# A fused attention and long-convolution kernel: SBUF laid out on two stacks, work paired anew, DRAM writes moved to another queue

## The chip, the cores and the metric

The program runs on one core of one Trainium2 chip. The time is device time in microseconds (us) of one execution. All executions counted here were fast; two slow ones are left out. Each kernel was timed in at least three rounds beside the kernel before, on the same chip. The engines are called PE (TensorE, matrix products), DVE (VectorE), ACT (ScalarE), POOL (GpSimd) and SP (SyncE, which here only issues DMAs). PEld is the loading of PE's weights, which overlaps its products.

## The reference

Two independent halves are computed and joined. Sequence length S is 2048, width D is 576, everything in bf16.

```python
def A(x, wqkv, wo):                 # 32 heads of 18; 8 taps, 2 apart
    q, k, v = split_heads(x @ wqkv)
    kg, vg = k[:, :, idx], v[:, :, idx]        # idx = pos - 2 * (0..7)
    logits = einsum("bhsd,bhswd->bhsw", q, kg) * scale   # masked where idx < 0
    o = einsum("bhsw,bhswd->bhsd", softmax(logits), vg)
    return merge_heads(o) @ wo

def B(q, k, v, shift_k, ssm_k, ssm_D):
    kv = short_conv_4_taps(k, shift_k) * v
    y = irfft(rfft(kv, 2S) * rfft(ssm_k, 2S))[:S]   # a long convolution
    return q * (y + kv * ssm_D)

return concatenate([A(...), B(...)], axis=-1)
```

## The kernel before

The kernel writes both halves as *steps* and emits them in pairs with `run(a, b)`, which interleaves two lists of steps. A scheduler at compile time then fixes the order of instructions on every engine; at run time each engine executes its own list strictly in that order, waiting where an input isn't there yet.

The steps that matter are these.

- `v_step` (16 of them) and `qk_step` (18 with the two half steps) project x: PE, then one ACT copy out of PSUM.
- `k_step` (8) makes the first half of the Fourier transform of the kernel `ssm_k`: PE transposes, one DVE copy into `kTt`, products (`L262`), ACT copies, and a write to DRAM (`Dk`).
- `x_step` (8): the four-tap convolution on DVE (`kv_step`, which makes `tA` for two x steps), then the same products, to `Dx`.
- `logit_step` (8): q times shifted k on DVE (`prod`), summed by head on PE, then one ACT copy (`Lsb`).
- `g_step` (8): reads `Dk` and `Dx`, second half of both transforms (`Kc`, `Xc`), their complex product on DVE (`m`), first half of the inverse transform, written to `Dy`.
- `pv_step` (8): attention weights times v on DVE (`P`), sum and output projection on PE.
- `y_step` (8): reads `Dy`, last half of the inverse transform, times q, output.

```python
    vX = const.tile([128, 30, D], BF16, name="vX")
    ...
    nc.gpsimd.memset(vX[0:1, 0:14, :], 0.0)                  # one partition
    ...
        # end of s1_chunk, the tail of k_step and x_step
        for ri in range(2):
            nc.scalar.dma_start(by_f1(Dd)[:, ri, 2 * c2:2 * c2 + 2, :], vst[...])
    ...
    permute_wv()                                             # on GpSimd
    a_steps = v steps + q/k steps
    run(a_steps[0:12], [k_step(c2) for c2 in range(8)])
    kpre_v.release(); kpre.release()
    kvp = pool("kvp", 2, "right")           # the convolution's buffers lie here
    run(a_steps[12:], [sk_step] + [x_step(c2) for c2 in range(8)])
    ...
    run([logit_step(wi) for wi in range(W)] + [softmax_step]
        + [at_step(wp) for wp in range(4)],
        [ia_tables] + [g_step(g) for g in range(3)])
    ...
    run([pv_step(tp) for tp in range(5)], [g_step(g) for g in range(3, 8)])
    run([pv_step(tp) for tp in range(5, 8)], [y_step(c2) for c2 in range(8)])
```

The convolution's buffers are allocated on the space that the `k_step` buffers give back. This is the point that the change is about.

## Time and profile before

The median is 333.05 us (332.08 to 333.26). The table of windows cuts the profiled execution (span 330.3 us) into stages; each engine's column is its busy time in that stretch, and the last three columns are the clock granted to PE (1.00 is full), the busy share of the DMA engines, and GB/s. Stages of the kernel before: set-up; v beside k steps; the k steps run out; convolution; logits with three g steps; softmax; PV; tail.

```profile
core 0: us, PE busy (x) PEld busy (x) DVE busy (x) ACT busy (x) POOL busy (x), PEclk, DMA share, GB/s
0.00:27.00 27.00, 9.63 (x81) 8.41 (x82) 21.27 (x30) 6.81 (x7) 19.95 (x32) 0.92 0.62 200
27.00:70.00 43.00, 40.18 (x290) 32.98 (x290) 6.06 (x8) 26.34 (x38) 0.00 (x0) 0.97 0.38 131
70.00:88.00 18.00, 16.84 (x77) 7.73 (x79) 1.36 (x1) 8.82 (x10) 1.53 (x1) 1.00 0.92 275
88.00:123.00 35.00, 29.54 (x154) 13.66 (x154) 34.02 (x26) 20.52 (x25) 0.00 (x0) 0.95 0.60 204
123.00:180.00 57.00, 34.37 (x319) 13.14 (x318) 55.02 (x42) 23.43 (x37) 2.85 (x4) 0.73 0.42 133
180.00:205.00 25.00, 12.13 (x96) 7.45 (x96) 21.24 (x19) 18.19 (x27) 9.33 (x20) 0.66 0.43 127
205.00:289.00 84.00, 76.11 (x909) 54.16 (x909) 57.40 (x35) 53.18 (x88) 0.00 (x0) 0.98 0.30 100
289.00:330.00 41.00, 23.12 (x207) 16.13 (x204) 13.98 (x17) 5.67 (x9) 3.26 (x6) 0.83 0.77 245
```

Read it down the PE and DVE columns. From 27 to 88 us PE is busy 57 of 61 us and DVE 7.4. From 123 to 180 us it is the other way round: DVE is busy 55 of 57 us, PE 34, and at a granted clock of 0.73. The Trainium skill ("TensorE: Matmul & The Clock Gate", What's actually happening) says that PE's clock is throttled by default and that activity releases it; from 27 us on the table agrees: 0.73 and 0.66 where PE is busy 34 of 57 and 12 of 25 us, 0.97 to 1.00 where it is busy 57 of 61. The two engines take turns, and the sum of the turns is the time.

A word on the clock column. Each figure is a mean over stretches recorded at 1.00 or 0.50, and time without a record counts as 1.00. The set-up's figures are therefore no measurement: the first record comes at 19.2 us here.

The waits of DVE from 27 to 125 us say why it idles. The columns are the engine, what it wants to run, what it waits for, then total us, times and the longest.

```profile
DVE kTt L288 <- PE psB L285: 34.8, 8, 11.0
DVE skb L326 <- DMA tB<-in_B_shift_k_dram: 16.9, 1, 16.9
```

The first convolution instruction, the copy of `shift_k` (`skb`), comes after all eight k steps, and then waits 16.9 us more for its load, which could be issued only when the k steps' buffers were free.

The set-up has a smaller oddity, seen in the timelines of DVE (first line) and of GpSimd (second line): start, duration, instruction.

```profile
4.94 6.81 DVE L138 TENSOR_SCALAR n_132<-g_130,p_f 128x128 int32<-128x128 int32 x2
```

```profile
4.76 6.84 POOL L191 MEMSET vX<- 1x8064 bf16 x1
```

A table instruction of 128x128 elements takes as long as the clearing of 8064 elements in one partition on another engine.

### The profile page before, as it was taken

To read this page: it belongs to the slowest core of one execution; us is meant where nothing else is said; L and a number is where in the kernel's file an instruction comes from. 1 tells how busy PE (TensorE), PEld (TensorE's weight loads), DVE (VectorE), ACT (ScalarE), POOL (GpSimd) and SP (SyncE) were. 2 spreads that over 40 slices of the span, in tenths; PEclk is the share of its full clock that TensorE was granted. 3 is DMA by queue.
4 is the path that set the end of the run, shared out by engine and by line. 5 is a ranking of instruction groups with operands and counts; after the bars stand their busy time and mean duration, and the time that the engine had idled before them with its cause. 6 is when DMAs were issued, how large, how long until landed. Compare 5 with 4: busy or idle time off the path is not lost.

```text
span 330.3 us, 5054 instructions
## 1 busy us (share of the span) xinstructions
PE 241.9 (73%) x2125; PEld 153.7 (47%) x2129; DVE 210.3 (64%) x175; ACT 163.0 (49%) x236; POOL 36.9 (11%) x61
## 2 busy tenths in 40 slices
PE   2349999879997874385657166999998978876732
PEld 2237876744443331032213034775766555665411
DVE  5981011100499999999997888977558663733431
ACT  1223567764446664072527587457756668431200
POOL 9950000010000000000004900000000000001110
PEclk9987999999997997569858557799999999999965
DMA  7907044459927836029604542162524201159993
GB/s 267 274 23 269 0 145 143 146 198 267 354 51 256 286 127 193 21 81 296 197 2 143 144 135 91 73 163 105 165 109 144 109 36 73 38 167 334 302 302 113
DMA packets 28355, 52.36 MB, mean 159 GB/s; under 512 B 2286, under 2 KB 22446, under 8 KB 28205
## 3 DMA queue, kind: packets, MB, share of 16 engines
q1 hardware_dynamic: 16156, 33.53, 32.1%
q10 hardware_dynamic: 10912, 15.34, 12.7%
q0 software_dynamic: 1264, 3.17, 3.8%
q8 instruction: 16, 0.26, 0.3%
q14 instruction: 7, 0.06, 0.0%
HBM read 31.11 MB, written 18.87 MB: 151 GB/s over the span
## 4 chain that ended last, share of the span: by engine, by line
issue 38%; DVE 26%; PE 15%; DMA 11%; ACT 4%; POOL 3%; SPq 1%; DVEq 0%; POOLq 0%
DVE prod L377 6%; PE psA L218 4%; DVE tB L343 4%; DVE tA L348 4%; DMA qt<-in_B_q_dram 3%; ACT vst L266 3%; PE psB L262 3%; DMA kX<-in_B_k_dram 3%; PE psB L285 2%; DVE n_132 L138 2%; DMA Wk<-Dy 2%; DVE W_73 L167 2%; DVE tA L343 2%; DVE stageB L543 2%; PE psA L202 1%
## 5 line engine op out<-in xcount | busy, mean ns | idle before, releaser
L505 DVE TENSOR_TENSOR P<-vX,at 128x4608 bf16<-128x4608 bf16 x16 | 40.3, 2554 | 20.6 <-PE psA L514 19.4
L514 PE MATMUL psA<-ident,P 128*128 128x128 bf16 (+1 forms) x640 | 46.3, 222 | 0.0
L266 ACT ACTIVATE vst<-psB 128x768 bf16<-128x768 f32 x48 | 36.6, 810 | 17.9 <-PE psB L262 17.3
L514 PEld LDWEIGHTS <-P 128*128 128x128 bf16 (+1 forms) x640 | 38.6, 101 | 9.7 <-issue 7.5
L231 PE MATMUL psA<-xT,wq 128*128 128x512 bf16 x156 | 37.1, 387 | 2.4 <-ACT vX L220 1.4
L288 DVE COPY kTt<-psB 128x1152 bf16<-128x1152 bf16 x8 | 6.1, 757 | 34.8 <-PE psB L285 34.8
L481 ACT ACTIVATE Y<-psB 128x576 bf16<-128x576 f32 x32 | 19.1, 652 | 16.3 <-PE psB L478 16.3
L536 POOL DMA_DIRECT2D qt<-in_B_q_dram x8 | 4.3, 544 | 201.3 <-DVE stageB L543 120.9
L543 DVE TENSOR_TENSOR stageB<-psB,qt 128x576 bf16<-128x576 f32 x16 | 11.4, 753 | 22.9 <-PE psB L542 10.4
L527 PE MATMUL psA<-wot,oT 128*128 128x288 bf16 x160 | 22.8, 287 | 3.9 <-ACT oT L520 3.0
L218 PE MATMUL psA<-wv,xT 128*128 128x288 bf16 x160 | 24.2, 297 | 1.9 <-ACT vX L220 1.3
L231 PEld LDWEIGHTS <-wq 128*128 128x128 bf16 x160 | 15.9, 99 | 20.8 <-issue 3.3
L380 PE MATMUL psA<-prod,Eh 128*32 128x512 bf16 x128 | 14.2, 489 | 14.8 <-DVE prod L377 14.7
L435 ACT ACTIVATE Kc<-psB 128x576 bf16<-128x576 f32 x32 | 19.8, 649 | 6.4 <-PE psB L432 3.9
L542 PE MATMUL psB<-Wk,IB 128*128 128x288 bf16 x64 | 12.9, 323 | 13.5 <-DMA Wk<-Dy 11.9
L432 PEld LDWEIGHTS <-W_73 128*64 128x64 bf16 x256 | 14.2, 116 | 17.5 <-issue 15.2
L218 PEld LDWEIGHTS <-xT 128*128 128x128 bf16 x160 | 20.4, 146 | 3.5 <-ACT xT L205 0.9
L202 PE MATMUL psA<-ident,xnat 128*128 128x128 bf16 x80 | 9.5, 304 | 16.8 <-DVE xT L207 10.0
L435 ACT ACTIVATE Xc<-psB 128x576 bf16<-128x576 f32 x32 | 19.7, 651 | 1.6 <-PE psB L432 1.3
L527 PEld LDWEIGHTS <-oT 128*128 128x128 bf16 x160 | 14.6, 98 | 10.2 <-ACT oT L520 4.1
L377 DVE TENSOR_TENSOR prod<-q_0_83,k_0_85 128x4096 bf16<-128x4096 bf16 x8 | 18.3, 2284 | 0.3 <-PE psA L380 0.2
L377 DVE TENSOR_TENSOR prod<-q_1_84,k_1_86 128x4096 bf16<-128x4096 bf16 x8 | 18.2, 2281 | 0.0
(164 smaller groups left out, 392.6 us busy)
## 6 DMA issues: line engine op xcount, KB each, us to landing
Dk<-vst ACTq DMA_DIRECT2D x16, 288.0 KB, 2.6
Dx<-vst ACTq DMA_DIRECT2D x16, 288.0 KB, 2.6
Wk<-Dk SPq DMA_DIRECT2D x8, 576.0 KB, 3.7
Wx<-Dx SPq DMA_DIRECT2D x8, 576.0 KB, 3.9
Dy<-Y ACTq DMA_DIRECT2D x8, 576.0 KB, 2.8
Wk<-Dy SPq DMA_DIRECT2D x16, 288.0 KB, 4.9
kX<-in_B_k_dram SPq DMA_DIRECT2D x3, 1008.0 KB, 5.5
vt<-in_B_v_dram SPq DMA_DIRECT2D x4, 576.0 KB, 7.5
```

Of the source, the lines that this page charges most:

```text
L218: nc.tensor.matmul(ps[:, di, 0:288], xTt[:, kb, t2, :], wv[:, kb, d0:d1], start=(kb == 0), stop=(kb == 4))
L231: nc.tensor.matmul(ps[:, u, :], wcols(kb, comp, ct), xT[:, kb, 512 * j:512 * j + 512], start=(kb == 0), stop=(kb == 4))
L266: nc.scalar.activation(vst[:, :, 384 * ch:384 * ch + 384], ps[:, :, 0:384], ACT.Copy)
L343: nc.vector.tensor_tensor(dst[:], kX[:, 3 - j:7 - j, :], skb[:, j, :].unsqueeze(1).to_broadcast([128, 4, D]), ALU.mult)
L377: nc.vector.tensor_tensor(prod[:], q2[ct // 2][:], k2[ct // 2][:, :, sh:sh + S], ALU.mult)
L380: nc.tensor.matmul(psw[32 * j:32 * j + 32, 0, :].rearrange("p (a b) -> p a b", b=4), Eh[:, ct, :], pr[:, :, 4 * j:4 * j + 4], start=(ct == ...
L435: nc.scalar.activation(dst[:, :, prl, d0:d1], ps[:, :, 0:288], ACT.Copy, scale=scale)
L481: nc.scalar.activation(Y[:, 2 * prl:2 * prl + 2, d0:d1], ps[:, :, 0:288], ACT.Copy)
L505: nc.vector.tensor_tensor(P[:].rearrange("p w (d h) -> p w d h", h=H), vs, at[:, :, t2, :].unsqueeze(2).to_broadcast([128, W, DH, H]), ALU ...
L514: nc.tensor.matmul(oacc[0:csz, ci, 128 * u:128 * u + 128], Ps[u][:, wi, 128 * ct:128 * ct + csz], ident[:], start=(ci % 2 == 0 and u == 0 ...
L527: nc.tensor.matmul(pso[:, di, 0:288], oT[:, ct, t2, :], wot[:, ct, d0:d1], start=(ct == 0), stop=(ct == 4))
L543: nc.vector.tensor_tensor(stage[:, u, :].rearrange("p (i d) -> p i d", i=2), ps[:, :, 0:288], qt[:, u, :].rearrange("p (i d) -> p i d", i= ...
```

## The change

The intent: let SBUF hold the convolution's buffers and the k steps' buffers at once, by giving the pools two stacks ("left" and "right") and by reusing dead tiles. Then the convolution (DVE) can run beside the q/k projections (PE), and the v projection and the kernel spectra (PE) beside the logits (DVE). The writes to DRAM move from the ACT queue to the SyncE queue, two DMAs become one, the softmax is cut in halves, and the clearing of `vX` becomes a small DMA that copies later rows there (`vX[0, 16:30]`): these taps are masked, their weight is zero, and any finite value will do.

```diff
@@ the layout of Dd on the way to DRAM, one DMA in place of two, another queue
-    def by_f1(Dd):
-        return Dd.rearrange("(r t) f d -> f r t d", r=2)
+    def by_f1(Dd, c2):
+        return Dd.rearrange("r f d -> f r d")[:, 4 * c2:4 * c2 + 4, :]
...
-        for ri in range(2):
-            nc.scalar.dma_start(by_f1(Dd)[:, ri, 2 * c2:2 * c2 + 2, :], ...)
+        nc.sync.dma_start(by_f1(Dd, c2), vst[:].rearrange("p r (t d) -> p (r t) d", t=2))
...
-        nc.scalar.dma_start(by_rt(Dy)[:, 4 * g:4 * g + 4, :], Y[:])
+        nc.sync.dma_start(by_rt(Dy)[:, 4 * g:4 * g + 4, :], Y[:])
@@ set-up: weights of q and k first, no clearing of vX
-    nc.gpsimd.memset(vX[0:1, 0:14, :], 0.0)
...
+    sk_step()                    # load and copy of shift_k, ahead of the rest
+    load_w(2, nc.sync)           # the weights of v
@@ stage 1: q/k beside x and k steps in turn
-    run(a_steps[0:12], [lambda c2=c2: k_step(c2) for c2 in range(8)])
-    kpre_v.release()
-    kpre.release()
-    kvp = pool("kvp", 2, "right")
-    run(a_steps[12:], [sk_step] + [lambda c2=c2: x_step(c2) for c2 in range(8)])
+    b_steps = [lambda c2=c2: x_step(c2) for c2 in range(8)]
+    for c2 in range(8):
+        b_steps.insert(2 * c2 + 1, lambda c2=c2: k_step(c2))
+    run(qk_steps, b_steps)
+    permute_wv()                 # now five copies on ACT
@@ stage 2: logits beside v and the kernel spectra (the Kc half of a g step)
+    def kh_step(g):
+        Wk = wk.tile([128, 4, D], BF16, name="Wk")
+        nc.sync.dma_start(Wk[:], by_rt(Dk)[:, 4 * g:4 * g + 4, :])
+        s2(Wk, g, Khat[:, :, 2 * g:2 * g + 2, :], 1.0 / 2048)
...
+    mixed = []
+    for g in range(8):
+        mixed += v_steps[2 * g:2 * g + 2] + [lambda g=g: kh_step(g)]
-    run([logit steps, softmax_step, at steps], [ia_tables, three g steps])
+    run([lambda wi=wi: logit_step(wi) for wi in range(W)], [ia_tables] + mixed + [halo])
@@ softmax in halves, then PV
+    softmax_a(0)
+    softmax_a(1)
+    g_step(0)
+    softmax_b(0)
+    softmax_b(1)
+    run([lambda wp=wp: at_step(wp) for wp in range(4)], [lambda: g_step(1)])
...
-    run([pv_step 0..4], [g_step 3..7])
-    run([pv_step 5..7], [y_step 0..7])
+    run([lambda tp=tp: pv_step(tp) for tp in range(4)], [lambda g=g: g_step(g) for g in range(2, 8)])
+    run([lambda tp=tp: pv_step(tp) for tp in range(4, 8)], [lambda c2=c2: y_step(c2) for c2 in range(8)])
```

The hunk headings and the last removed lines are shortened; pools, renamed buffers and the softmax bodies are cut. Cut too are a new order of the q/k steps (`jp` outermost) and the table code for the new layout of `Dd`.

## The prediction

> What bounds the kernel now. The table of windows shows six stages. 0-27 us: set-up; TensorE (PE) waits for transposes whose copies VectorE (DVE) starts only at 12.7 us, because its first table op ran 6.7 us against a 6.8 us one-partition GpSimd memset of vX. The Trainium skill ("SBUF — State Buffer", shared port pair) describes such blocking; the timeline agrees (both end at 11.7 us). 27-123 us: PE-bound, about 93% busy (v beside k steps, then q/k); DVE is nearly idle until 88 us (7.4 of 61 us busy): the convolution's buffers come free only when the k steps end. 123-177 us: DVE-bound (53.7 of 54 us: rest of the convolution, logit products at 2.28 us, three g steps), PE only 32 of 54 busy at a granted clock of 0.72. 177-205: softmax; first P product at 204.9. 205-292: PE-bound, 7 PV steps and five full g steps. The last Dy write is issued at 289.4; then 41 us of tail limited by DMA (about full share, 302-334 GB/s at 300-320 us).
>
> What changes. Work is re-paired: convolution (DVE 43 us) and k steps beside q/k (PE); v projection and kernel spectra (PE) beside the logits (DVE).
>
> Costs, from durations in the trace:
> - Set-up: the vX memset and the 5.3 us GpSimd wv copy go. But DVE's order puts the shift_k copy ahead of the first x-transpose copy; its load took 11.7 us here and now queues behind x and weights, landing near 16 us. ScalarE (ACT) holds wv copies, waiting for the v weights, ahead of its transpose copies. I expect q/k matmuls to start near 32 us, against 26.8 for the first projection now: +5 us.
> - Stage 1: 200 q/k matmuls x 0.213 us = 43 us, k steps 8 x 2.2, x steps 8 x 1.0: 69 us of PE, about 75 with gaps. DVE needs 51, ACT 57, so both fit. End near 107 us.
> - Stage 2: DVE 8 x 5.24 + 3 = 45 us; PE v 18, kernel spectra 15.4, logits about 13 (17.8 at clock 0.72 now), tables 2.5: 49 us, about 52 with gaps, at a higher clock because PE no longer idles. End near 158, now 178. The gain: about 20 us.
> - Softmax in halves overlaps Exp with DVE, no g-step products between: about 21 us from last logit to first P instead of 25-26. P starts near 180.
> - Last stages: 7 g steps without the kernel's half (3.6 us PE each) cost what five full ones (5.7) did; 84 us to the last Dy write, then the same DMA-bound tail: the same Dy, q and output bytes remain, in rows of 1152 bytes. Fewer DMAs, and writes on the SyncE queue, save issue time: under 2 us. The Trainium skill ("DMA: Bandwidth & Descriptors", Issuing engines are not separate DMA queues) says issuing from another engine saves only sequencer time; the trace shows 0.33-0.5 us an issue.
>
> Sum: 180 + 84 + 41 = 305; I put 308 us, range 294 to 324. Chances: faster 0.88, within 2% 0.09, slower 0.03.
>
> What shows it right: DVE busy from about 32 us in the table of windows; last logit product at 150-162; granted clock near 1.0 in the logit stage; first P at 172-188; last Dy write to end 37-43 us.
>
> What would make it wrong: the convolution's k and v loads landing well after 33 us, so PE waits at the first x step; the logit products holding one of two psA buffers, serialising the v steps; DVE, with seven g steps, limiting the PV stage; the shift_k copy landing past 20 us.

## The result, and the profile after

The changed kernel takes 307.9 us (307.36 to 310.15, four runs) against 333.15 us (332.08 to 334.75, four runs). The ratio is 0.925 (95% interval 0.919 to 0.931). Ratios here are the mean time of one kernel's fast runs over the mean of the other's of the same rounds, so they are not quite the ratios of the medians quoted. The profiled execution has a span of 308.4 us. Its table of windows, with the columns of the table before; the stages are set-up, stage 1 (q/k beside convolution and k steps, two lines), stage 2 (logits), softmax, PV, tail:

```profile
0.00:29.00 29.00, 9.59 (x80) 8.52 (x81) 12.30 (x34) 12.23 (x12) 8.74 (x31) 1.00 0.96 305
29.00:92.00 63.00, 62.68 (x339) 30.31 (x338) 47.13 (x39) 44.49 (x56) 0.00 (x0) 1.00 0.53 188
92.00:103.00 11.00, 9.24 (x66) 6.52 (x65) 3.57 (x3) 9.11 (x15) 0.00 (x0) 1.00 0.56 196
103.00:151.00 48.00, 45.43 (x494) 28.03 (x493) 41.18 (x30) 33.04 (x56) 4.04 (x6) 1.00 0.42 128
151.00:177.00 26.00, 5.09 (x48) 3.92 (x48) 16.89 (x23) 11.38 (x15) 7.09 (x15) 0.67 0.55 144
177.00:264.00 87.00, 79.98 (x924) 54.13 (x924) 68.34 (x46) 51.44 (x86) 1.09 (x2) 0.94 0.32 110
264.00:308.00 44.00, 24.85 (x182) 15.96 (x180) 12.11 (x17) 4.29 (x8) 3.23 (x6) 0.68 0.71 228
```

From 29 to 92 us PE is busy 62.7 of 63 us while DVE does 47 us of convolution beside it. In the logit stage both work (45 and 41 of 48 us), at the full clock. That is the intent, seen. The events of the two timelines say where the 22 us of the two profiled spans come from (the medians differ by 25 us):

| event, us from the start | before | after | gained by then |
|---|---|---|---|
| first projection product | 26.8 | 29.1 | -2.3 |
| last copy of logits (`Lsb`) done | 179.7 | 150.8 | 28.9 |
| first P | 204.9 | 176.5 | 28.4 |
| last write of `Dy` issued | 289.4 | 264.1 | 25.3 |
| end of the span | 330.3 | 308.4 | 21.9 |

All the gain, and more, is made in stages 1 and 2. After that 7 us go back: 3 in PV and 3.5 in the tail.

The set-up's DVE and ACT waits after, 0 to 30 us:

```profile
DVE skb L315 <- DMA tB<-in_B_shift_k_dram: 10.3, 1, 10.3
ACT wv L298 <- DMA wq<-in_A_wqkv_dram: 8.6, 1, 8.6
```

The copy of `shift_k` stands first in DVE's list and the copies of the v weights first in ACT's, and both wait for late loads, as predicted; they end at 16 and 18 us. Answering to the odd pair of before, the table instruction now takes 0.48 us for two, as the DVE timeline after has it:

```profile
4.82 0.48 DVE L163 TENSOR_SCALAR n<-g,p_f 128x128 int32<-128x128 int32 x2
```

The softmax stage did not shrink: 25.7 us from the last logits to the first P, against 25.2 before. DVE's timeline after, around its end:

```profile
166.01 1.23 DVE L426 TENSOR_TENSOR Lsb<-Lsb,mx 128x2048 bf16<-128x2048 bf16 x1
173.94 1.36 DVE L477 TENSOR_TENSOR m<-Xc,Khat 128x2304 bf16<-128x2304 bf16 x1 [6.70 <-ACT Xc L448]
175.21 1.35 DVE L478 TENSOR_TENSOR m<-Xc,Khat 128x2304 bf16<-128x2304 bf16 x1
176.48 2.55 DVE L532 TENSOR_TENSOR P<-vX,at 128x4608 bf16<-128x4608 bf16 x1
```

The softmax proper ends at 167.2 us. DVE then waits 6.70 us for `Xc` of the first g step and makes two of its products before the first P. ACT's timeline says why `Xc` is late: it stands behind six copies of the transposed weights, which could start only when the softmax was done.

```profile
168.37 3.27 ACT L435 ACTIVATE at<-psA 128x512 bf16<-128x512 bf16 x6 [8.76 <-PE psA L433]
171.53 2.37 ACT L448 ACTIVATE Xc<-psB 128x576 bf16<-128x576 f32 x4
```

### The profile page after: what moved, and what is told of

Read it like the earlier page. It is cut to its first block, busy times and chain, and to the rows that moved or that the text cites. A ratio compares the mean times of both kernels' runs of the same rounds, so it can differ in the third digit from the quotient of the medians.

```text
span 308.4 us, 5069 instructions
## 1 busy us (share of the span) xinstructions
PE 236.9 (77%) x2129; PEld 147.4 (48%) x2129; DVE 201.5 (65%) x188; ACT 166.0 (54%) x242; POOL 24.2 (8%) x59
## 4 chain that ended last, share of the span: by engine, by line
PE 49%; DVE 15%; DMA 14%; ACT 11%; issue 9%; SPq 0%; POOL 0%; DVEq 0%; ACTq 0%; POOLq 0%
PE psA L246 11%; PE psB L445 7%; PE psA L233 6%; PE psB L277 6%; DMA wq<-in_A_wqkv_dram 5%; DMA Xc<-in_B_q_dram 5%; PE psA L541 4%; DVE P L532 3%; PE psB L290 3%; PE psA L554 3%; PE psB L487 3%; PE psA L388 3%; ACT Y L490 3%; DMA Wx<-Dy 2%; DVE m L478 2%
## 5 line engine op out<-in xcount | busy, mean ns | idle before, releaser
L385 DVE TENSOR_TENSOR prod<-q,k 128x4096 bf16<-128x4096 bf16 x16 | 36.0, 2287 | 2.0 <-PE psA L388 2.0
L570 DVE TENSOR_TENSOR Y<-psB,Xc 128x576 bf16<-128x576 f32 x16 | 11.6, 754 | 29.0 <-PE psB L569 16.7
L554 PE MATMUL psA<-wv,xT 128*128 128x288 bf16 x160 | 25.8, 292 | 1.6 <-ACT xT L547 1.5
L569 PE MATMUL psB<-Wx,IB 128*128 128x288 bf16 x64 | 14.9, 404 | 15.3 <-DMA Wx<-Dy 15.2
L233 PE MATMUL psA<-wv,xT 128*128 128x288 bf16 x160 | 24.6, 292 | 0.2 <-ACT vX L235 0.2
L233 PEld LDWEIGHTS <-xT 128*128 128x128 bf16 x160 | 19.4, 145 | 4.7 <-issue 4.3
L448 ACT ACTIVATE Khat<-psB 128x576 bf16<-128x576 f32 x32 | 19.7, 650 | 3.5 <-PE psB L445 3.0
L554 PEld LDWEIGHTS <-xT 128*128 128x128 bf16 x160 | 13.7, 99 | 10.8 <-issue 4.5
L524 POOL DMA_DIRECT2D wv<-in_A_wo_dram x18 | 8.9, 500 | 125.6 <-PE psA L233 119.8
L569 PEld LDWEIGHTS <-IB 128*128 128x128 bf16 x64 | 7.8, 130 | 21.8 <-DMA Wx<-Dy 16.1
L293 DVE COPY kTt<-psB 128x1152 bf16<-128x1152 bf16 x8 | 6.1, 758 | 18.4 <-PE psB L290 18.3
L477 DVE TENSOR_TENSOR m<-Xc,Khat 128x2304 bf16<-128x2304 bf16 x8 | 10.8, 1356 | 10.9 <-ACT Xc L448 10.9
L144 PEld LDWEIGHTS <-xnat 128*128 128x128 bf16 x80 | 8.4, 144 | 19.9 <-issue 13.5
```

What stands on the lines that cost most here:

```text
L233: nc.tensor.matmul(ps[:, di, 0:288], xTt[:, kb, t2, :], wv[:, kb, d0:d1], start=(kb == 0), stop=(kb == 4))
L385: nc.vector.tensor_tensor(prod[:], q2[ct // 2][:], k2[ct // 2][:, :, sh:sh + S], ALU.mult)
L448: nc.scalar.activation(dst[:, :, prl, d0:d1], ps[:, :, 0:288], ACT.Copy, scale=scale)
L554: nc.tensor.matmul(pso[:, di, 0:288], oT[:, ct, t2, :], wot[:, ct, d0:d1], start=(ct == 0), stop=(ct == 4))
L569: nc.tensor.matmul(ps[:, di, 0:288], IB[:, ri, :], Vy[:, ri, u, d0:d1], start=(ri == 0), stop=(ri == 1))
```

## The experiments

The theory at the start: the gain comes from the new pairs of stages 1 and 2, and the rest (set-up, queue, fewer DMAs) is worth little. The rivals: only one of the pairs does it; the missing `vX` memset does it; the queue does it. Event times are of the profiled execution of each kernel; the totals are medians, and "before" is the kernel before, run in the same rounds.

### The queue of the writes back to ACT

```diff
-        nc.sync.dma_start(by_f1(Dd, c2), vst[...])
+        nc.scalar.dma_start(by_f1(Dd, c2), vst[...])
-        nc.sync.dma_start(by_rt(Dy)[...], Y[:])
+        nc.scalar.dma_start(by_rt(Dy)[...], Y[:])
```

> The changed kernel with its DRAM writes (Dk, Dx, Dy) issued by ScalarE again. Theory (the gain is the new pairing of DVE work with PE work): within 2 us of 308, ratio to before 0.92 to 0.935. Rival (the writes on the SyncE queue made the gain): 318 us or more, with ScalarE's copies visibly delayed in the q/k stage.

Measured: 331.15 us (330.9 to 331.29), ratio to before 0.993 (0.990 to 0.997). Nearly the whole gain is gone with two words. The last copy of logits is at 162.4 us instead of 150.8, the last `Dy` write at 289.5 instead of 264.1. An issue on ACT takes 0.33 to 0.38 us in the trace and there are 24 of them, about 9 us of ACT in all; that does not make 23 us of span, the less as ACT is busy only about half of the time. So the theory had missed something, and this run alone does not say what: the built program also has another order of instructions on PE, DVE and ACT, though the source of those is the same.

### The memset of vX taken out of the kernel before

```diff
-    nc.gpsimd.memset(vX[0:1, 0:14, :], 0.0)
...
     nc.sync.dma_start(vX[113:128, 0:14, :], vX[112:127, 16:30, :])
+    nc.sync.dma_start(vX[0:1, 0:14, :], vX[0:1, 16:30, :])
```

> The kernel before without the one-partition GpSimd memset of vX (row copied by DMA instead). Theory (pairing): the first projection starts 3 to 5 us earlier than 26.8 us and the total falls by about 4 us, to 327-331. Rival (set-up blocking made the gain): falls by 10 us or more, to 323 or less.

Measured: 331.94 us (331.01 to 333.75), ratio 0.997 (0.992 to 1.003), so no difference is shown. The projection starts at 26.0 us instead of 26.8. In this kernel's timeline the two table instructions take 0.29 and 0.34 us instead of 6.6 and 6.7. DVE's busy time in the set-up falls from 21.3 to 11.4 us, but the time turns into a wait, as the table of waits from 0 to 27 us shows:

```profile
DVE Eh L180 <- POOL e_f L79: 8.5, 1, 8.5
```

The memset was real as a cost of one instruction, and worth under 1 us at the start of the projection: another wait stood right behind it.

### The v projection back beside q/k

```diff
-    run(qk_steps, b_steps)
     permute_wv()
+    run(v_steps + qk_steps, b_steps)
...
-        mixed += v_steps[2 * g:2 * g + 2] + [lambda g=g: kh_step(g)]
+        mixed += [lambda g=g: kh_step(g)]
```

> The changed kernel with the 16 v steps back beside q/k, only the kernel spectra left beside the logits. Theory: the PE-bound first stage grows by the v work, about 20 us; the logit stage becomes DVE-bound at about 45 us instead of 48; total 320 to 326 us, and the granted clock in the logit stage stays high or drops without moving the total. Rival (only the place of the convolution matters): 306 to 311 us.

Measured: 321.58 us (320.95 to 322.45), ratio 0.965 (0.961 to 0.968), 13.7 us above the changed kernel's 307.9. The first `prod` is at 119.6 us instead of 100.9, and the last copy of logits at 168.0 instead of 150.8. Stage 1 and stage 2 of this kernel in its table of windows:

```profile
29.00:119.00 90.00, 86.91 (x531) 55.19 (x537) 48.00 (x41) 60.58 (x81) 10.59 (x20) 1.00 0.57 183
119.00:168.00 49.00, 34.15 (x360) 14.05 (x359) 43.84 (x30) 25.82 (x43) 0.57 (x1) 0.85 0.40 122
```

The 18.7 us that stage 1 is longer are PE work: PE is busy 87 of 90 us. Stage 2 takes 48.4 us with 34 us of PE work in it, and 49.9 us in the changed kernel with 45. So the v projection is almost free beside the logits and costs its full length beside q/k. This run settles that pair, since the stages, not only the totals, show it. Some 4 us of the loss come back later.

### The convolution after q/k and k steps

```diff
-    for c2 in range(8):
-        b_steps.insert(2 * c2 + 1, lambda c2=c2: k_step(c2))
-    run(qk_steps, b_steps)
+    run(qk_steps, [lambda c2=c2: k_step(c2) for c2 in range(8)])
+    run(b_steps, [])
```

> The changed kernel with the eight convolution steps emitted after q/k and the k steps; two of four convolution chunks then come on DVE after q/k. Theory: about 20 us of DVE work is no longer beside PE-bound work and lands in front of the DVE-bound logits: total 324 to 332 us, last logit product about 20 us later. Rival (the place of v alone, or queues, made the gain): 306 to 312 us.

Measured: 330.73 us (329.24 to 332.49), ratio 0.992 (0.986 to 0.998), 22.8 us above the changed kernel. The first `prod` comes earlier (86.9 us), the last copy of logits at 173.3 us: 86.4 us for stage 2. The stretch after the q/k products, where the second half of the convolution shares DVE with the first logit products, in the table of windows:

```profile
100.00:120.00 20.00, 6.74 (x40) 2.30 (x38) 19.63 (x17) 6.47 (x9) 0.00 (x0) 0.60 0.20 73
```

DVE 19.6 of 20 us, PE 6.7, the clock at 0.60: the picture of the kernel before. The other pair matters too. This run also has another compile-time order: from 120 to 140 us neither engine is full (PE 12.8, DVE 6.9 of 20 us). So the 22.8 us are not all the bare cost of DVE work; the run shows the pair's worth roughly, not to the microsecond.

Each of the two undone pairs costs more than half of the gain, and together more than all of it, so the two costs are not independent shares. What remained was the queue.

### Queue and order apart

The next two kernels fix the order of PE, DVE and ACT instructions by ordering edges, which add no waits of their own. The first has the writes on the ACT queue and the order of the changed kernel. The second has the writes on the SyncE queue and the order that the compile step had made for the ACT queue.

```diff
+    pin_order(tc)      # one edge from each PE, DVE, ACT instruction to the next
```

> DRAM writes issued by ScalarE, as in e1_actq, but with every matrix, vector and scalar instruction pinned to the order it has in the changed kernel; only the place of the 24 write issues differs from it. If the loss of e1_actq came from the compile-time order of the compute instructions, which changed with the queue: 307 to 313 us. If it came from the issues themselves, which took 0.33 to 0.38 us each on ScalarE in e1_actq: about 325 to 331 us.

> The converse: DRAM writes on the SyncE queue, but matrix, vector and scalar instructions pinned to the order of e1_actq. If the order is the cause: 325 to 332 us. If the issues are: 307 to 312 us.

Measured, with the two earlier kernels:

| median us | order made for SyncE | order made for ACT |
|---|---|---|
| writes on SyncE | 307.9 (the changed kernel) | 330.73 (329.71 to 332.2) |
| writes on ACT | 309.76 (308.41 to 310.79) | 331.15 |

The ratios to before are 0.925 and 0.990 in the first row, 0.927 and 0.993 in the second. Down a column the queue is worth 0 to 2 us, within the intervals. Along a row the order is worth 21 to 23 us. As far as these runs can tell, the queue acts through the order made at compile time alone: the prediction was right about what an issue costs while running and did not think of the order.

What is wrong with the other order? The waits of PE in stage 1 (29 us to the first logits), first in the changed kernel, then with writes and order of ACT, then with the writes on SyncE in the order of ACT:

```profile
PE psB L277 <- DVE kTt L293: 1.1, 2, 0.9
```

```profile
PE psB L277 <- DVE kTt L293: 6.4, 6, 1.6
```

```profile
PE psB L277 <- DVE kTt L293: 6.7, 6, 1.7
```

The timelines of PE and DVE show how such a wait comes about. A k step's transposes (`L290`) need a DVE copy (`L293`) before its products (`L277` on `kTt`) can run. First the changed kernel, then the one with the writes on ACT; the last line of each is from DVE's timeline:

```profile
63.80 1.17 PE L290 MATMUL psB<-ident,knat 128*128 128x128 bf16 x10
64.91 1.68 PE L246 MATMUL psA<-xT,wq 128*128 128x512 bf16 x7
66.43 0.81 PE L277 MATMUL psB<-kTt,T 128*128 128x384 bf16 x4
65.01 0.76 DVE L293 COPY kTt<-psB 128x1152 bf16<-128x1152 bf16 x1 [0.29 <-PE psB L290]
```

```profile
65.62 1.18 PE L290 MATMUL psB<-ident,knat 128*128 128x128 bf16 x10
66.97 0.81 PE L246 MATMUL psA<-xT,wq 128*128 128x512 bf16 x3 [0.18 <-ACT q L249]
69.18 0.81 PE L277 MATMUL psB<-kTt,T 128*128 128x384 bf16 x4 [1.40 <-DVE kTt L293]
68.38 0.75 DVE L293 COPY kTt<-psB 128x1152 bf16<-128x1152 bf16 x1
```

In the changed kernel the copy starts as soon as the transposes end, and seven q/k products cover it. In the other kernel the transposes end at 66.80 us, but DVE's list has two convolution instructions (1.36 and 1.35 us) ahead of the copy. It starts 1.6 us late, and PE stands still for 1.40 us; at the next k step the same costs 1.61 us. At the last four k steps no product stands between transposes and use, and PE waits 0.85 us each time, though the copy starts at once; in the changed kernel that happens once. The first `prod` is 8.5 us later. The waits for `kTt` make 5.3 us of that; all waits of PE in the stage are 9.5 us against 2.2.

The second part is in the PV stage: 101.4 us from the first P to the last `Dy` write instead of 87.6. PE waits there longer for the products of the g steps (`m`) and for ACT's copies ahead of the output projection (`L554`); first in the changed kernel, then with writes and order of ACT:

```profile
PE psB L487 <- DVE m L479: 1.7, 4, 0.5
PE psA L554 <- ACT xT L547: 1.3, 2, 0.7
```

```profile
PE psA L554 <- ACT xT L545: 6.7, 4, 1.7
PE psB L487 <- DVE m L479: 6.1, 6, 1.5
```

All waits of PE in the stage are 20.9 us against 9.2, which is 11.7 of the 13.8 us. The order made for ACT does not undo the pairs: its last copy of logits, at 162.4 us, is still 17.3 us ahead of the kernel before. It loses most of that again in PV.

The sum agrees with the spans: 11.6 us up to the last copy of logits, 13.8 in PV, 4.6 back in the tail, together 20.8, the difference of 329.2 and 308.4. Why the compile step chose that order is not shown by any run; only that it did and what the chip made of it.

### The queue alone in the kernel before

```diff
-            nc.scalar.dma_start(by_f1(Dd)[:, ri, ...], vst[...])
+            nc.sync.dma_start(by_f1(Dd)[:, ri, ...], vst[...])
-        nc.scalar.dma_start(by_rt(Dy)[...], Y[:])
+        nc.sync.dma_start(by_rt(Dy)[...], Y[:])
```

> The kernel before with only its DRAM writes moved to the SyncE queue, the order left to the scheduler. Pairing as the main cause: 326 to 336 us, because its DVE-bound stretch from 88 us on is untouched. Queue as a cause of its own: 322 us or less.

Measured: 340.11 us (339.11 to 341.11), ratio 1.018 (1.015 to 1.022): slower by 6 us than the 334.14 of the same rounds. That is clear of the noise, but as it lies about the bound of 2% the verdict on record is "unclear". Both expected ranges were missed; nobody had thought of a loss. Its last logit product ends at 183.3 us instead of 178.1. The queue as such is not a gain, then; with these steps the program comes out slower. The two traces show different orders here too (DVE's list differs in 55 of 175 places, ACT's in 69 of 236). How much of the 6 us is order and how much is the SyncE queue was not taken apart here, as it was for the changed kernel.

### Towards a better version: the g steps in a software pipeline

In the PV stage of the changed kernel the g steps run about 12 us apart, one to a PV step: `s2(g)`, products on DVE, inverse transform of g, and only then `s2(g+1)`, all through one ring of two PSUM buffers. In the next kernel `s2(g+1)` is emitted before the inverse transform of g, all eight g steps stand beside three PV steps, and the y steps beside the other five.

```diff
+    def g_a(g):            # load of Wx, s2 into Xc
...
         m products of g
+        if g < 7:
+            xcs[g + 1] = g_a(g + 1)
         inverse transform of g, write to Dy
...
-    run([pv_step 0..3], [g_step 2..7])
-    run([pv_step 4..7], [y_step 0..7])
+    run([pv_step 0..2], [g_step 0..7])
+    run([pv_step 3..7], [y_step 0..7])
```

> The changed kernel with the g steps software-pipelined (the first spectrum of step g+1 is emitted between the products and the inverse of step g; eight steps beside three PV steps, the y steps beside the other five). If the 44 us after the last Dy write are a DMA-bound tail that only lacked PE work beside it: last Dy write before 250 us, end 285 to 298 us. If the tail is bound by something else, or the g steps by the order on DVE: 303 to 310 us.

Measured: 287.0 us (286.48 to 288.49), ratio 0.859 (0.857 to 0.862). That is 21 us below the changed kernel. The last `Dy` write comes at 233.9 us instead of 264.1. The last two stages in the table of windows:

```profile
178.00:234.00 56.00, 51.71 (x545) 31.64 (x546) 51.13 (x39) 41.20 (x69) 1.09 (x2) 0.91 0.45 154
234.00:285.00 51.00, 43.37 (x547) 37.35 (x543) 28.66 (x23) 13.46 (x20) 3.22 (x6) 1.00 0.68 215
```

Against the changed kernel's 79.98 of 87 us and 24.85 of 44 us: the reads of `Dy` and the output now overlap with PE work that used to stand before them, and PE keeps its clock (1.00 against 0.68) in the tail. The first branch of the expectation came true. Of the 640 products of P on PE, the changed kernel makes 560 before the last `Dy` write and 80 after it, this one 260 and 380. So PV work that had kept `Dy` late now fills the tail, where PE waits 2.7 us for `Dy` instead of 15.2. The run changes two things at once, the pipelining and the split of the steps. No run has one alone; that PE waited only 2.0 us for the g steps' `m` and `Y` in the changed kernel's PV stage speaks for the split.

### The set-up in another order

```diff
-    sk_step()
-    load_w(2, nc.sync)
+    sk_step()              # its DVE copy held behind the last copy of x
+    loaded[0] = kv_load(0) # first k and v rows ahead of the kernel rows
...
+    load_w(2, nc.sync)     # v weights after the kernel rows
...
+    qk_steps.insert(12, wv_step)   # ACT copies of the v weights in mid-stage
```

> The kernel of e8_gpipe3 with the set-up put in another order: the copy of shift_k stands behind the last x copy on VectorE instead of ahead of them, the first k and v rows are loaded ahead of the kernel rows, the v weights are loaded after the kernel rows, and the ScalarE copies of the v weights stand in the middle of stage 1. Theory 1 (the start of stage 1 is set by the two copies that stand first in line and wait for late loads: shift_k at 16.0 us on VectorE, v weights until 17.9 us on ScalarE): first q/k products at 18 to 22 us instead of 29.2, everything after it earlier by as much, total 277 to 283 us. Rival (the loads themselves bound it, the copies only hid that): first q/k products at 27 to 29 us, total 285 to 288 us (e8_gpipe3: 287.0).

Measured: 286.59 us (284.97 to 288.46, three fast runs), ratio 0.860 (0.852 to 0.867): nothing gained that can be shown, although the first half of theory 1 came true: the first q/k product is at 18.7 us instead of 29.3. The first `prod` is at 102.0 us in both. The chain of waits of this kernel from 28 us to the first logits starts with these lines (start, length, what):

```profile
19.82 12.15 DMA kX<-in_B_k_dram
31.99 1.36 DVE tA L343
33.35 1.28 DVE tA L348
34.65 1.37 DVE tA L349
36.06 1.44 PE psB L283 x4
```

PE gets 10 us ahead and then has to stop for the first x step, whose k rows land at 32 us; from 10 to 30 us the DMA engines' share is 1.04 in its table of windows, so they are full. A stretch of the table of windows shows where PE then idles (5.74 of 10 us busy, against 9.94 in the pipelined kernel; from 70 to 80 us it is 7.36 against 9.86):

```profile
30.00:40.00 10.00, 5.74 (x23) 2.49 (x23) 7.91 (x6) 3.59 (x5) 0.00 (x0) 0.83 0.58 218
```

The set-up theory falls as a theory of the total. The rival as written ("the loads bound the start of q/k") falls too; loads bound, but at the first convolution step. What the stage needed early, by this chain, was the k rows as well as x and weights.

### The first g step held ahead of the transposes

```diff
     xcs[0] = g_a(0)
+    s2_pe, s2_act = last_on(PE_), last_on(ACT_)
...
+    with tc.issue_after(s2_pe), tc.issue_after(s2_act):
         for wp in range(4):
             at_step(wp)
```

> The kernel of e8_gpipe3 with the first convolution group's Wx products and their ScalarE evacuations held ahead of the transposes of the logits and their copies, by ordering edges alone. Theory 1 (between the last logits and the first P, VectorE waits 6.7 us for a ScalarE evacuation that stands behind six copies of transposes): last logit evacuation to first P 19 to 22 us instead of 25.7, total 282 to 286 us. Rival (the wait only moves, the softmax itself takes the 25 us): 25 us again, total 286.5 to 288 us.

Measured: 281.44 us (280.12 to 282.15), ratio 0.844 (0.840 to 0.847), 5.6 us below the pipelined kernel by the medians (they ran on different chips; the intervals of their ratios to before, 0.857 to 0.862 there, do not overlap). From the last copy of logits to the first P it takes 22.5 us, against 25.7. That is just above the 19 to 22 expected, but the total is where theory 1 had it. DVE's timeline, around the end of the softmax:

```profile
166.46 1.22 DVE L431 TENSOR_TENSOR Lsb<-Lsb,mx 128x2048 bf16<-128x2048 bf16 x1
167.61 1.35 DVE L487 TENSOR_TENSOR m<-Xc,Khat 128x2304 bf16<-128x2304 bf16 x1
173.85 2.56 DVE L547 TENSOR_TENSOR P<-vX,at 128x4608 bf16<-128x4608 bf16 x1 [2.16 <-ACT at L440]
```

The products of g follow the softmax without a wait (the 6.70 us are gone), all four are made before the first P instead of two, and 2.16 us of another wait appear. The other part of the gain is in PV: 53.1 us to the last `Dy` write instead of 56.4.

### Both edits

> Both edits on e8_gpipe3. If both theories hold, the gains add, for they lie in different stages: total 273 to 280 us, first q/k products at 18 to 22 us. If the compile-time order of the q/k stage turns out worse by the set-up edit, the stage from first q/k products to the last logit evacuation (122.6 us in e8_gpipe3) is longer, and the total is above 285 us.

Measured: 278.99 us (278.87 to 281.81, three fast runs), ratio 0.839 (0.834 to 0.845). The first q/k product is at 20.0 us, the first `prod` at 101.1. The total lies in the range given for gains that add, but the interval overlaps with that of the run before, so the set-up edit again adds nothing that can be shown. The stage from the first q/k product to the last logits is 130.8 us instead of 122.6: what the start gained is lost there. The version with the least time is this one or the one before it, 16% below the kernel before and 9% below the changed kernel.

What the move of the spectra alone is worth stays open.

## Why the prediction was right or wrong

The total was right: 308 us predicted, 307.9 measured. The parts were not all right, and they cancelled. The marks of the prediction were 32, 158, 180, 264 and 305 us; the trace has 29.1, 150.8, 176.5, 264.1 and 308.4.

- **Set-up: right in its mechanism.** "landing near 16 us" for `shift_k`: its copy ran at 15.99 us. ACT was held until 17.9 us by the v weights. The start was 29.1, not 32. Neither bounds the total, as the set-up experiment showed on the pipelined kernel; the prediction counted its 5 us as a cost of the total.
- **Stages 1 and 2: right.** 126 us predicted from the first q/k product to the last logit, 121.6 measured. The gain there was 28.9 us, where about 20 had been predicted. (Its "PE-bound" from 27 to 123 us fits up to 88 us only; from there on DVE is busy 34.0 of 35 us and PE 29.5.) PE bound in stage 1 (62.7 of 63 us), full clock in stage 2. Undoing either pair cost 13.7 and 22.8 us. The sign "last logit product 150-162" was missed by 3 us on the good side (147.2).
- **Softmax: wrong.** The failing step is "no g-step products between: about 21 us from last logit to first P". It took 25.7. Two g-step products do stand before the first P, and DVE waits 6.70 us for them. The run that held the g step's copies ahead brought it to 22.5.
- **PV and tail: right in kind, small in size.** 84 us and 41 us predicted, 87.6 and 44.3 measured; the tail's sign (37 to 43) was missed. The prediction had named no cause for more, and none is shown for these few us. What it did not see is how much the stage could give: with seven eighths of P's products ahead of the last `Dy` write, PE waited 15.2 us for `Dy` in the tail; pipelining the g steps, together with the new split of the steps, took 21 us off.
- **Queue: the sentence held, the question was wrong.** "Fewer DMAs, and writes on the SyncE queue, save issue time: under 2 us." With the order held fixed the queue is worth 0 to 2 us (the smaller number of DMAs was not tested alone). The Trainium skill ("DMA: Bandwidth & Descriptors", Issuing engines are not separate DMA queues) says just this of the sequencer's time, and the runs agree. But the queue decided which of two orders the compile step made, and that is worth 21 to 23 us. Had the order come out the other way, the same change would have measured 331 us, outside the predicted range; the prediction took no account of that. That it came out this way was luck.
- **The memset.** The Trainium skill ("SBUF — State Buffer", Who interferes with whom) says that DVE and GpSimd can exclude each other on one pair of ports. The trace agrees (6.81 us of DVE beside 6.84 us of GpSimd, and 0.29 to 0.34 us an instruction without it). The prediction used it rightly as a cost of the instruction. Its worth in the total was within the noise.

## What to carry to other kernels

Look for stages in which two engines take turns; pairing their work can hide what the less busy one does there (here 18.7 us of stage 1 for the v projection), and the proof is one undone pair at a time, read by stage. Where a compile step orders the instructions, any edit, even of a DMA's queue, may change two things: fix the order in both directions (new queue with old order, old queue with new order) before giving the gain to the edit. And before an early wait is removed, ask what the same engine waits for next: the memset here gave under 1 us at the first product and the set-up order 10 us there, and neither gave anything at the end.

## What the Trainium skill lacked or had wrong

- "DMA: Bandwidth & Descriptors", Issuing engines are not separate DMA queues: right for what happens at run time (0.33 to 0.38 us an issue on ACT; 0 to 2 us in the total with the order held). It lacks a warning that choosing the issuing engine may change the compile-time order of the compute engines; here that was 21 to 23 us of 308, and 6 us the other way for the queue in the kernel before (there not taken apart).
- "SBUF — State Buffer", Who interferes with whom: right; it quotes a slowdown without its instructions, and no duration for this pair. Measured: an instruction of 128x128 int32 takes 6.6 to 6.7 us beside a one-partition clearing of 8064 bf16 on GpSimd, and 0.29 to 0.34 us without. The table instruction of `W` (128x4096) took 5.80 us beside a GpSimd copy before and 2.29 us after.
- "TensorE: Matmul & The Clock Gate": agrees with the tables here from the first projection on (there is no clock record before); the granted clock was 0.60 where PE was busy 6.7 of 20 us, and 1.00 where it was busy 62.7 of 63.
- No page that I used has a rule for how far apart in a PE list a transpose and the use of its evacuated result should stand. Here four to ten instructions between them cost 0.21 us or nothing when the 0.76 us DVE copy started at once, and none cost 0.85 us. Where DVE had two convolution instructions ahead of the copy, three and five between them still left waits of 1.40 and 1.61 us, so the place in DVE's list counts as well.
